# Routing attention and a bilinear feed-forward block: Strassen products for two thirds of the first batch element's up-projection, weight checks on ScalarE

## The chip, the cores and the metric

The kernel runs on one core of one Trainium2 chip. Its time is the device time in microseconds, the median of repeated runs. Before the change it is 1047.72 us (three runs, 1047.59 to 1048.28). The profile is of one execution with a span of 1045.6 us. The core has five engines with a queue each, which run side by side and wait for each other by semaphores: TensorE (PE in the profile, its weight loads PEld), VectorE (DVE), ScalarE (ACT), GpSimd (POOL) and SyncE (SP, which issues transfers here). Within a queue, instructions are worked off in order.

## What is computed

Cut to what matters, the reference is:

```python
# q, k, v: (4, 8, 768, 64), centroids: (8, 16, 64)
mask   = argmax(q_n @ c_n) [:, :, :, None] == argmax(k_n @ c_n) [:, :, None, :]
scores = where(mask, 0.125 * q @ k^T, -1e9)
attn   = softmax(scores)                      # per batch element and head
x      = (attn @ v) as (3072, 512)            # rows: batch and position
out    = ((x @ w_a) * (x @ w_b)) @ w_out      # w_a, w_b: 512 x 1536, w_out: 1536 x 512
```

The weights arrive as 64-bit floats. The kernel makes 32-bit floats of them on the chip, from the two 32-bit halves of each number.

## The kernel before

**Attention.** Four batch elements with four pairs of heads each make 16 pairs (`p`). A pair has 12 units (two halves `hf` of 384 queries, six blocks `j` of 128 keys), and two units are one group `g`, so a pair lasts 6 groups and the loop over `g` in `short_path` runs 96 of them. A group's own work is `score` (one-hot products that make the mask and q-k products into the same bank, L556), `exp` on ScalarE (L565), and, one group later, `add_up` (running sums of the exponentials, L586) and `weigh` (products with `v`, L597). Every third group `denominators` sums the exponentials over the partitions on TensorE (L620), and `normalize` inverts them (VectorE, L640 to L647) and multiplies `xT` by them (GpSimd, L652). Exponentials lie in four buffers (`pt`), scores in two.

**Clusters of the next pair.** `prep_steps` spreads them over the 6 groups of the current pair. From the fifth pair on (`by_blocks`) they are made without TensorE's transposes: VectorE transposes q and k (L477), TensorE makes the similarities in `prep_sim` (L373), VectorE transposes these (`sims_across`, L481), finds the first largest one (`assign`, L502 to L507), VectorE and GpSimd make the one-hot rows (L489, L487), VectorE transposes them (L493), and eight transfers put them into `ohT` (L497), which `score` of the pair reads.

**Feed-forward block.** For a batch element, `xT` is 512 x 768 (transposed), in four chunks of 128 and two halves of 384 columns. The up-projection makes 12 blocks `f` of 128 features. For batch elements 1 to 3, `ffn_ups` makes it by Strassen's method (Winograd's form): two blocks of features, two halves of the channels and two halves of the columns are a 2 x 2 by 2 x 2 product with seven products in place of eight. Each product is one piece of four matmuls, and each set of seven needs four combinations of weights on VectorE (S1 to S4, two chunks each, L782), four combinations of `xT` for the whole batch element (T1 to T4, L755, L767), four additions on VectorE (L815), three or four copies on ScalarE (L812) and, in every second set, three multiplications on GpSimd (L821) and one on VectorE (L864). The first batch element's up-projection is made in the plain way by `ffn_block`: a piece is eight matmuls, with one copy on ScalarE for `w_a` (L705) and one multiplication on VectorE for `w_b` (L709). `ffn_downs` (Strassen too) makes the down-projection. Matmuls of all pieces are issued at L678; the trace holds two records for each.

**Order.** The order of all queues is written out by the loop: in a group come `score`, `add_up`, the flush, `weigh`, the denominators, a step of the clusters, the rounding that is due, and then pieces of the feed-forward queue `ffn` until a credit of columns (`PER_GROUP`) is used up. After every piece one VectorE step from `todo` and one rounding that is due are put in. The first four pairs run without pieces, since no `xT` is complete yet. At the end of group 22 the first half of the first batch element is ready, and its first eight pieces are put in the queue; the others follow at the end of group 25.

**Weights.** 36 parts of 128 x 512 are loaded (two buffers `raw`). `round_w` makes a part by four VectorE instructions (L280 to L290), a size on ScalarE (L294) and an addition on GpSimd (L295). In the next group `flush_w` multiplies the part by "size at least `SMALLEST`" on VectorE (L302), which sets to zero what is too small. `due` says which part is rounded in which group: eight in the first 22 groups, the others from group 23 on, three in two groups.

**Check at the end.** `stat` holds what must stay below `LIMIT`; where it doesn't, a second program (`long_path`) computes attention again.

Of the kernel before, what the change touches and what calls it, by code (L numbers as in the profile page):

```python
# [28 lines left out]
SMALLEST = 1.125 * 2.0 ** -15  # L29

# [5 lines left out]
def kernel(  # L36
# [97 lines left out]
    with tc.If(redo > 0):  # L134
        with ExitStack() as slow:
            long_path(nc, tc, slow, c, q, k, v, out)


def short_path(nc, tc, ctx, c, cn, centroids_in, casts, n_far, q, k, v,
# [32 lines left out]
    sizep = pool("sizep", 2)  # L172
# [96 lines left out]
    flush = []  # L269

    def round_w(i):
        flush_w()
        w = w_parts[i][0]
        wi = w.bitcast(INT32)
        raw = raws.pop(i)
        halves = lambda dt: raw.bitcast(dt).rearrange("p (n two) -> p n two", two=2)
        lo, hi = halves(UINT32)[:, :, 0], halves(INT32)[:, :, 1]


        nc.vector.tensor_scalar(out=wi, in0=hi, scalar1=3, scalar2=0x3FFFFFF8,  # L280
                                op0=ALU.logical_shift_left,
                                op1=ALU.bitwise_and)
        nc.vector.scalar_tensor_tensor(out=wi, in0=hi, scalar=SIGN_TOP, in1=wi,
                                       op0=ALU.bitwise_and, op1=ALU.bitwise_or)

        rest = wtp.tile([P, WN], FP32, name="rest")
        nc.vector.tensor_scalar(out=rest.bitcast(INT32), in0=wi,
                                scalar1=SIGN_EXP, scalar2=None,
                                op0=ALU.bitwise_and)
        nc.vector.scalar_tensor_tensor(out=rest, in0=lo, scalar=2.0 ** -52,  # L290
                                       in1=rest, op0=ALU.mult, op1=ALU.mult)

        size = sizep.tile([P, WN], FP32, name="size")
        nc.scalar.activation(out=size, in_=halves(FP32)[:, :, 1], func=AF.Abs)  # L294
        nc.gpsimd.tensor_tensor(out=w, in0=w, in1=rest, op=ALU.add)  # L295
        flush.append((w, size))

    def flush_w():

        while flush:  # L300
            w, size = flush.pop(0)
            nc.vector.scalar_tensor_tensor(out=w, in0=size, scalar=SMALLEST,  # L302
                                           in1=w, op0=ALU.is_ge, op1=ALU.mult)

    stat = zero.tile([P, 4 * NPAIR], FP32, name="stat")
# [42 lines left out]
    def prep_transpose(p, i):  # L348
        if i == 0:
            qkTs[p] = qtp.tile([P, 2 * S], FP32, name="qkT")  # L350
        ps = ps_m.tile([P, 512], FP32, name="m")
        for n in range(4):
            w, j = divmod(4 * i + n, NJ)
            nc.tensor.transpose(  # L354
                out=ps[:, n * P:(n + 1) * P],
                in_=qks[p][:, w, j].rearrange("p a d -> p (a d)"),
                identity=ident)
        dst = qkTs[p][:, i * 512:(i + 1) * 512]
        if p == 0 and i == 2:
            nc.vector.tensor_copy(out=dst[:, 0:256], in_=ps[:, 0:256])  # L360
            nc.scalar.copy(out=dst[:, 256:], in_=ps[:, 256:])
        elif p == 0 and i != 1 or p == 1 and i == 2:
            nc.vector.tensor_copy(out=dst, in_=ps)
        else:
            nc.scalar.copy(out=dst, in_=ps)
# [94 lines left out]
    def prep_by_blocks(p):  # L460
# [47 lines left out]
        if p == HP:  # L508
            return [[lambda: across(0), lambda: across(1)], [sims_across],
                    assign[:2], assign[2:], [one_hot, one_hot_across], []]  # L510
# [3 lines left out]
    def prep_steps(p):  # L514
# [6 lines left out]
        if by_blocks(p):  # L521
            steps = prep_by_blocks(p)
            ready = [lambda s=s: todo.extend(s) for s in steps]
            ready[1] = both(lambda: prep_sim(p), lambda: load_v(p), ready[1])
            return ready
# [50 lines left out]
    def add_up(u):  # L576
# [6 lines left out]
        for a in range(2):  # L583
            many = p >= HP and (a == 1 or j in (2, 4))
            eng = nc.gpsimd if many else nc.vector
            eng.tensor_tensor(  # L586
                out=acc[:, a, :],
                in0=probs[u - 1][:, a, :] if j == 1 else acc[:, a, :],
                in1=probs[u][:, a, :], op=ALU.add)
# [97 lines left out]
    def ffn_block(b, blk):  # L687

        box = {}
        t0 = blk * HB  # L690

        def up(w_sb, f):
            ps = in_turn()
            for ch in range(NCH):
                in_halves(ps[:, 0:HB], w_sb[:, ch, f * P:(f + 1) * P],
                          xTs[b][:, ch, t0:t0 + HB],
# [3 lines left out]
        def piece_a(f):  # L700
            if f == 0:
                box["h"] = hp_.tile([P, NF, HB], FP32, name="h")
            ps = up(wa_sb, f)
            box["a"] = hap.tile([P, HB], FP32, name="ha")
            nc.scalar.copy(out=box["a"], in_=ps[:, 0:HB])  # L705

        def piece_b(f):
            ps = up(wb_sb, f)
            nc.vector.tensor_tensor(out=box["h"][:, f, :], in0=box["a"],  # L709
                                    in1=ps[:, 0:HB], op=ALU.mult)  # L710

        ups = [(NCH * HB, lambda f=f, piece=piece: piece(f))
               for f in range(NF) for piece in (piece_a, piece_b)]
        return ups, box
# [11 lines left out]
    def room():  # L726
        if not W:
            W["raw"] = [rawp.tile([P, 2 * WN], FP32, name="raw") for _ in range(2)]
            W["size"] = [sizep.tile([P, WN], FP32, name="size") for _ in range(2)]
            W["comb"] = combp.tile([P, 2 * P], FP32, name="comb")  # L730
        return W["raw"], W["size"], W["comb"]
# [4 lines left out]
    def up_room():  # L736
        raw, size, comb = room()
        quarter = lambda t: t[:, 0:2 * HB].rearrange("p (c t) -> p c t", c=2)
        beside = lambda t: t[:, 2 * HB:].rearrange("p (c f) -> p c f", c=2)
        chunks = lambda t: [t[:, c, :] for c in range(2)]  # L740
        W["T3"], W["T2"] = chunks(quarter(raw[0])), chunks(quarter(raw[1]))
        W["T4"] = [t[:, 0:HB] for t in size]
        W["slots"] = [chunks(beside(raw[0])), chunks(beside(raw[1])),
                      chunks(comb.rearrange("p (c f) -> p c f", c=2)),
                      [t[:, HB:] for t in size]]

    def combine_x(b):
        up_room()
        x = xTs[b]
        for c in range(2):  # L750
            x11, x12 = x[:, c, 0:HB], x[:, c, HB:S]
            x22 = x[:, c + 2, HB:S]
            t2, t3 = W["T2"][c], W["T3"][c]
            for out, l, r in ((t3, x22, x12), (x12, x12, x11), (t2, x22, x12)):
                nc.vector.tensor_tensor(out=out, in0=l, in1=r, op=ALU.subtract)  # L755

    def ffn_ups(b, h):

        x = xTs[b]
        X = {"11": [x[:, c, 0:HB] for c in (0, 1)],  # L760
             "T1": [x[:, c, HB:S] for c in (0, 1)],
             "21": [x[:, c, 0:HB] for c in (2, 3)],
             "22": [x[:, c, HB:S] for c in (2, 3)]}

        def combine_t4():
            for c in range(2):
                nc.vector.tensor_tensor(out=W["T4"][c], in0=X["21"][c],  # L767
                                        in1=W["T2"][c], op=ALU.subtract)

        def products(w_sb, i, is_a):  # L770
            N2 = NF // 2
# [13 lines left out]
            def half_1():  # L785
                combine("S1", A["21"], A["22"], ALU.add)
                combine("S2", A["S1"], A["11"], ALU.subtract)

            def half_2():
# [20 lines left out]
            def take(name, k, f):  # L810
                box[name] = place(k, f)
                nc.scalar.copy(out=box[name], in_=box["X"][:, 0:HB])  # L812

# [53 lines left out]
            return half_1, half_2, [p1, p2, p6, p5, p7, p3, p4]  # L867

        parts = [products(w_sb, i, w_sb is wa_sb) for i in range(NF // 2)
                 for w_sb in (wa_sb, wb_sb)]  # L870
        pieces = []
        for n, (half_1, half_2, ps) in enumerate(parts):
            if n == 0:
                ps[0] = both(half_1, half_2, ps[0])
                ps[2] = both(combine_t4, ps[2])
            if n + 1 < len(parts):
                ps[4] = both(ps[4], parts[n + 1][0])
                ps[6] = both(ps[6], parts[n + 1][1])
            pieces += [(2 * HB, f) for f in ps]
        return pieces  # L880
# [9 lines left out]
    def ffn_downs(b, h):  # L890
# [97 lines left out]
        def before():  # L988
            down_room()
# [19 lines left out]
    blocks = {}  # L1009

    def ffn_ready(p, hf):

        b, hp = divmod(p, HP)
        if hp < HP - 1:
            return
        if b > 0:
            if hf == 0:
                return
            h = []
            ffn.insert(len(ffn) - FREE_ROOM, (0, lambda: combine_x(b)))  # L1020
            ffn.extend(ffn_ups(b, h) + ffn_downs(b, lambda: h))
        elif hf == 0:
            blocks[0] = ffn_block(0, 0)
            ffn.extend(blocks[0][0][0:8])
        else:
            ups0, box0 = blocks[0]
            ups, box = ffn_block(0, 1)
            for n in range(3):
                ffn.extend(ups[8 * n:8 * n + 8] + ups0[8 * n + 8:8 * n + 16])
            ffn.extend(ffn_downs(0, lambda: (box0["h"], box["h"])))  # L1030
# [3 lines left out]
    GPP = UPP // 2  # L1034
# [6 lines left out]
        (UP + DOWN * 7 / 8, BG + 5.8), ((UP + DOWN) * 7 / 8, BG + 0.8),  # L1041
# [7 lines left out]
    for i in range(8, len(w_parts)):  # L1049
        due.setdefault(23 + int((i - 8) / 1.5), []).append(i)  # L1050
# [4 lines left out]
    keep_busy(12)  # L1055
    prep_transpose(0, 0)
    prep_transpose(0, 1)
# [26 lines left out]
    for g in range(NG + 3):  # L1084
# [13 lines left out]
        flush_w()  # L1098
# [7 lines left out]
        parts = due.get(g, [])  # L1106

        def round_next():
            if parts:
                i = parts.pop(0)  # L1110
                round_w(i)
                load_w(i + 2)
# [42 lines left out]
    fine = zero.tile([P, 4 * NPAIR], FP32, name="fine")  # L1155
# [15 lines left out]
def long_path(nc, tc, ctx, c, q, k, v, out):  # L1171
# [20 lines left out]
    R = 2 * NC  # L1192

# [200 lines left out]
```

## Time and profile before

| | busy us | share of the span | instructions |
|---|---|---|---|
| TensorE, matmul | 1032.8 | 99% | 7163 |
| VectorE | 657.2 | 63% | 1314 |
| GpSimd | 329.9 | 32% | 311 |
| ScalarE | 303.1 | 29% | 590 |

The first row says which engine sets the time: on the page, the chain of work that ended last is TensorE for 93% of the span and VectorE for 4%. The other rows are averages over stages that differ, so the stretch that a change touches has to be asked for by itself. The groups of instructions give a mean duration for each line: an addition of two running sums on VectorE (L586) 802 ns, a combination of weights (L782) between 285 and 644 ns, an addition to a bank's result (L815) about 550 ns, the flush (L302) 880 to 1154 ns. "Idle before" in the same rows is the time that the engine waited and for whom.

### The profile page before, as it was taken

What the parts mean: (1) busy time and instruction counts of PE and PEld (TensorE: products, weight loads), DVE (VectorE), ACT (ScalarE), POOL (GpSimd) and SP (SyncE); (2) the same over time, 40 slices, a digit from 0 to 9 for tenths busy, and PEclk for the clock granted to TensorE, in tenths of its full rate; (3) what the DMA queues carried; (4) which work ended last, traced back from release to release, by engine and by line L of the source; (5) the groups of instructions that cost most, each with busy time, mean ns of one, the idle gap of its engine ahead of it and who ended that gap; (6) DMA issues with size and microseconds to landing.
All of it is one profiled execution on the core that took longest, in us unless ns stands there. A gap on an engine that the chain in (4) does not pass through costs nothing.

```text
span 1045.6 us, 17833 instructions
## 1 busy us (share of the span) xinstructions
PE 1032.8 (99%) x7163; PEld 502.6 (48%) x7163; DVE 657.2 (63%) x1314; ACT 303.1 (29%) x590; POOL 329.9 (32%) x311
## 2 busy tenths in 40 slices
PE   9999999999999999999999999999999999999997
PEld 5444444444445554444444555444444565444564
DVE  6778877887857447555556746765454845554652
ACT  5665333233322222333323122333232201111100
POOL 1111345455543322343442422443333310211100
PEclk9999999999999999999999999999999999999999
DMA  7334343526120121203020030300000000000001
GB/s 183 87 86 86 85 106 105 125 68 144 63 49 20 40 43 23 38 5 46 4 46 3 24 66 22 49 1 20 1 4 1 11 31 21 1 1 1 2 30 34
DMA packets 120521, 46.48 MB, mean 44 GB/s; under 512 B 106608, under 2 KB 115824, under 8 KB 120432
## 3 DMA queue, kind: packets, MB, share of 16 engines
q1 hardware_dynamic: 120016, 44.85, 18.8%
q8 instruction: 58, 0.95, 0.4%
q10 hardware_dynamic: 416, 0.43, 0.1%
q14 instruction: 31, 0.25, 0.1%
HBM read 37.78 MB, written 6.29 MB: 42 GB/s over the span
## 4 chain that ended last, share of the span: by engine, by line
PE 93%; DVE 4%; issue 1%; POOL 1%; ACT 0%; DMA 0%; DVEq 0%; POOLq 0%
PE m L678 62%; PE s L556 15%; PE O L597 12%; PE s L620 1%; PE s L373 1%; PE m L620 1%; DVE raw L755 1%; PE m L373 0%; POOL xT L652 0%; DVE xT L755 0%; DMA h<-in_q_dram 0%; PE m L354 0%; DVE comb L782 0%; DVE acc L586 0%; DVE acc L647 0%
## 5 line engine op out<-in xcount | busy, mean ns | idle before, releaser
L565 ACT ACTIVATE pt<-s 128x768 f32<-128x768 f32 x192 | 145.3, 808 | 206.5 <-PE s L556 161.7
L586 POOL TENSOR_TENSOR acc<-acc,pt 128x384 f32<-128x384 f32 x144 | 152.6, 1073 | 60.2 <-ACT pt L565 43.0
L597 PE MATMUL O<-pt,v 128*64 128x384 f32 x768 | 145.0, 499 | 0.0
L556 PE MATMUL s<-qkT 64*128 64x384 f32 x768 | 139.7, 482 | 0.0
L821 POOL TENSOR_TENSOR h<-h,ha 128x384 f32<-128x384 f32 x54 | 55.5, 1030 | 258.6 <-DVE ha L815 257.7
L678 PE MATMUL m<-xT,wa_sb 128*64 128x384 f32 x672 | 117.5, 487 | 2.7 <-DVE ha L815 1.0
L678 PE MATMUL m<-xT,wb_sb 128*64 128x384 f32 x672 | 116.9, 487 | 0.0
L815 DVE TENSOR_TENSOR ha<-ha,m 128x384 f32<-128x384 f32 x72 | 39.6, 550 | 98.0 <-PE m L678 75.4
L586 DVE TENSOR_TENSOR acc<-acc,pt 128x384 f32<-128x384 f32 x96 | 74.5, 802 | 36.6 <-POOL acc L586 35.5
L815 DVE TENSOR_TENSOR h<-h,m 128x384 f32<-128x384 f32 x72 | 39.5, 548 | 80.7 <-PE m L678 53.8
L812 ACT COPY h<-m 128x384 f32<-128x384 f32 x72 | 34.5, 479 | 184.9 <-PE m L678 184.9
L597 PEld LDWEIGHTS O<-pt,v 128*64 128x64 f32 x768 | 46.6, 136 | 85.8 <-issue 80.1
L678 PE MATMUL m<-wo_sb,h 128*64 128x256 f32 x768 | 86.7, 379 | 0.0
L556 PEld LDWEIGHTS s<-qkT 64*128 64x128 f32 x768 | 70.5, 187 | 31.3 <-issue 0.2
L678 PEld LDWEIGHTS m<-xT,wa_sb 128*64 128x64 f32 x672 | 48.7, 137 | 63.4 <-issue 53.3
L678 PE MATMUL m<-raw 128*64 128x384 f32 x432 | 78.9, 486 | 0.0
L652 POOL TENSOR_TENSOR xT<-xT,acc 128x384 f32<-128x384 f32 x32 | 32.8, 1026 | 144.9 <-DVE acc L647 144.6
L678 PEld LDWEIGHTS m<-xT,wb_sb 128*64 128x64 f32 x672 | 49.0, 137 | 60.1 <-issue 56.2
L678 PEld LDWEIGHTS m<-wo_sb,h 128*64 128x64 f32 x768 | 54.9, 137 | 31.1 <-issue 5.0
L678 PE MATMUL m<-xT,h 128*64 128x256 f32 x576 | 64.5, 379 | 0.0
L678 PE MATMUL m<-xT,size 128*64 128x384 f32 x288 | 52.7, 487 | 0.0
L678 PEld LDWEIGHTS m<-xT,h 128*64 128x64 f32 x576 | 41.3, 137 | 22.3 <-issue 2.3
(169 smaller groups left out, 1302.0 us busy)
## 6 DMA issues: line engine op xcount, KB each, us to landing
raw<-in_moe_w_a_dram SPq DMA_DIRECT2D x12, 512.0 KB, 3.8
raw<-in_moe_w_b_dram SPq DMA_DIRECT2D x12, 512.0 KB, 3.6
raw<-in_moe_w_out_dram SPq DMA_DIRECT2D x12, 512.0 KB, 3.7
qk<-in_q_dram SPq DMA_DIRECT2D x48, 96.0 KB, 3.1
qk<-in_k_dram SPq DMA_DIRECT2D x48, 96.0 KB, 3.6
v<-in_v_dram SPq DMA_DIRECT2D x24, 192.0 KB, 3.8
out_dram<-rest SPq DMA_DIRECT2D x24, 128.0 KB, 1.7
v<-in_v_dram SPq DMA_DIRECT2D x4, 384.0 KB, 4.5
```

Source lines behind the costliest of these rows:

```text
L373: nc.tensor.matmul(out=ps[32 * kq:32 * kq + 32, 0:HB], lhsT=cTb[:, hp, :], rhs=qkTs[p][:, kq * HB:(kq + 1) * HB], start=True, stop=True)
L556: nc.tensor.matmul(out=s[:, a, 0:HB], lhsT=Ts[p][r, S + j * P:S + (j + 1) * P], rhs=Ts[p][r, hf * HB:(hf + 1) * HB], start=start, stop=not ...
L565: nc.scalar.activation(out=pt, in_=s[:, :, 0:HB], func=AF.Exp, scale=SCALE)
L586: eng.tensor_tensor(out=acc[:, a, :], in0=probs[u - 1][:, a, :] if j == 1 else acc[:, a, :], in1=probs[u][:, a, :], op=ALU.add)
L597: nc.tensor.matmul(out=O_of[0][a * D:(a + 1) * D, 0:HB], lhsT=vs[p][:, a, j, :], rhs=probs[u][:, a, :], start=(j == 0), stop=(j == NJ - 1))
L620: nc.tensor.matmul(out=ps[a * D:(a + 1) * D, 0:HB], lhsT=ones, rhs=t[:, a, :], start=(n == 0), stop=(n == len(terms) - 1))
L652: nc.gpsimd.tensor_tensor(out=x, in0=x, in1=den, op=ALU.mult)
L678: nc.tensor.matmul(out=ps[half], lhsT=lhsT[:, half], rhs=rhs, **kw)
L755: nc.vector.tensor_tensor(out=out, in0=l, in1=r, op=ALU.subtract)
L812: nc.scalar.copy(out=box[name], in_=box["X"][:, 0:HB])
L815: nc.vector.tensor_tensor(out=box[name], in0=box[name], in1=box[bank][:, 0:HB], op=ALU.add)
L821: nc.gpsimd.tensor_tensor(out=to, in0=to, in1=box[name], op=ALU.mult)
```

## The change

It does seven things.

- **First batch element.** Blocks 0 to 7 of its up-projection are made by `ffn_ups` (pairs 0 with 2, 1 with 3, 4 with 6, 5 with 7; 8 sets of seven products), blocks 8 to 11 in the plain way (`plain_ups`). No piece starts before both halves are ready, so all of them follow at the end of group 25. T1 to T4 lie in parts of `h` that are written later, and most of them, with S1 to S4 of the first set, are made from group 14 to group 24 (`early_steps`); T2, T3 and T4 of the second chunk are made at the end of group 25.
- **Weight check.** The flush on VectorE goes. In its place ScalarE makes the size in BF16, and a second instruction (Relu, with an accumulator) puts the amount by which sizes fall short into `stat` (`see_w`). It is put behind ScalarE's copies, and the next part's load behind it. Zeroing is done by `long_path`, if at all.
- **Rounding.** Parts from the ninth on are due from group 25, 1.45 a group.
- **Clusters.** `sims_across` of pairs from the fifth on is put in at once instead of through `todo`, which places it in front of that group's rounding; for the fifth pair the one-hot rows are made a group sooner.
- **Sums.** Of the first head's sums, VectorE makes blocks 1, 2 and 3 and GpSimd 4 and 5. Before, VectorE made 1, 3 and 5 and GpSimd 2 and 4.
- **Start.** Five matmuls fewer that only keep TensorE busy, and the first copies of the transposes go to ScalarE, the last to VectorE.
- **Later batch elements.** The combinations of `xT` come in two steps instead of one, those of the weights in three instead of two.

```diff
+        unseen.append((i, halves(FP32)[:, :, 1]))
-    def flush_w():
-        while flush:
-            w, size = flush.pop(0)
-            nc.vector.scalar_tensor_tensor(out=w, in0=size, scalar=SMALLEST,
-                                           in1=w, op0=ALU.is_ge, op1=ALU.mult)
+    def see_w():
+        while unseen:
+            i, upper = unseen.pop()
+            size = spare()[1].bitcast(BF16)[:, WN:2 * WN]
+            nc.scalar.activation(out=size, in_=upper, func=AF.Abs)
+            n = 4 * NPAIR + i
+            nc.scalar.activation(out=size, in_=size, func=AF.Relu, scale=-STEEP,
+                                 bias=edge[:, 0:1], accum_out=stat[:, n:n + 1])
+            load_w(i + 2)
...
-        if p == 0 and i == 2:
-            nc.vector.tensor_copy(out=dst[:, 0:256], in_=ps[:, 0:256])
-            nc.scalar.copy(out=dst[:, 256:], in_=ps[:, 256:])
-        elif p == 0 and i != 1 or p == 1 and i == 2:
+        if p < 2 and i == 2:
             nc.vector.tensor_copy(out=dst, in_=ps)
...
         if p == HP:
-            return [[lambda: across(0), lambda: across(1)], [sims_across],
-                    assign[:2], assign[2:], [one_hot, one_hot_across], []]
+            return [[lambda: across(0), lambda: across(1)],
+                    [sims_across] + assign[:2], assign[2:] + [one_hot],
+                    [one_hot_across], [], []]
...
-            ready[1] = both(lambda: prep_sim(p), lambda: load_v(p), ready[1])
+            ready[1] = both(lambda: prep_sim(p), lambda: load_v(p), steps[1][0],
+                            lambda: todo.extend(steps[1][1:]))
...
-            many = p >= HP and (a == 1 or j in (2, 4))
+            many = p >= HP and (a == 1 or j > 3)
...
+        return {HP * GPP - 10: both(begin, T("T1", 0)), HP * GPP - 8: T("T1", 1),
+                HP * GPP - 4: T("T3", 0), HP * GPP - 3: T("T2", 0),
+                HP * GPP - 2: T("T4", 0),
+                HP * GPP - 1: lambda: [f() for f in combinations[0:2]],
+                HP * GPP: lambda: combinations[2]()}
...
-        elif hf == 0:
-            blocks[0] = ffn_block(0, 0)
-            ffn.extend(blocks[0][0][0:8])
         else:
-            ups0, box0 = blocks[0]
-            ups, box = ffn_block(0, 1)
-            for n in range(3):
-                ffn.extend(ups[8 * n:8 * n + 8] + ups0[8 * n + 8:8 * n + 16])
-            ffn.extend(ffn_downs(0, lambda: (box0["h"], box["h"])))
+            h = h_first
+            for name in ("T3", "T2", "T4"):
+                combination_x(0, name, 1)
+            ffn.extend(ups_first + plain_ups(0, h, range(NF - 4, NF)))
+        ffn.extend(ffn_downs(b, lambda: h))
...
-        (UP + DOWN * 7 / 8, BG + 5.8), ((UP + DOWN) * 7 / 8, BG + 0.8),
+        (UP * 11 / 12 + DOWN * 7 / 8, BG + 2.8), ((UP + DOWN) * 7 / 8, BG + 0.8),
...
-        due.setdefault(23 + int((i - 8) / 1.5), []).append(i)
+        due.setdefault(25 + int((i - 8) / 1.45), []).append(i)
...
-    keep_busy(12)
+    keep_busy(5)
     prep_transpose(0, 0)
+    keep_busy(2)
...
-        flush_w()
```

## The prediction

> **What bounds the kernel now.** I read the page's busy times and chain first, then the table of stages, then who waited in the stage that the change rebuilds. The page:
>
> ```profile
> PE 1032.8 (99%) x7163; PEld 502.6 (48%) x7163; DVE 657.2 (63%) x1314; ACT 303.1 (29%) x590; POOL 329.9 (32%) x311
> PE 93%; DVE 4%; issue 1%; POOL 1%; ACT 0%; DMA 0%; DVEq 0%; POOLq 0%
> ```
>
> TensorE is busy for all but 13 us and is 93% of the chain, so time comes from fewer matmuls or fewer waits of TensorE, and VectorE work counts only where TensorE waits for it. Three stages (us from the start: groups 21 to 25; the first batch element's feed-forward beside attention; the second's, by Strassen, beside attention):
>
> ```profile
> 97.30:139.30 42.00, 39.70 (x244) 18.27 (x244) 33.42 (x60) 16.79 (x32) 10.68 (x9) 1.00 0.42 101
> 139.30:302.50 163.20, 163.20 (x1022) 70.53 (x1023) 131.23 (x200) 55.71 (x105) 87.47 (x75) 1.00 0.34 90
> 398.80:560.70 161.90, 161.40 (x1016) 69.45 (x1016) 92.31 (x200) 50.10 (x98) 60.18 (x59) 1.00 0.16 26
> ```
>
> Columns: length, then busy PE, PEld, DVE, ACT, POOL. Only in the first does TensorE lose time; in the second VectorE is busy for 80%, with rounding and plain pieces; in the third 57%, with Strassen pieces and no rounding. The change puts Strassen pieces and rounding together. TensorE's waits in the first:
>
> ```profile
> PE s L556 <- DVE sim L481: 1.0, 1, 1.0
> PE m L678 <- POOL xT L652: 0.9, 1, 0.9
> ...
> PE s L620 <- DVE acc L586: 0.5, 1, 0.5
> ```
>
> With a 0.5 us wait that shows only on the weight load (below), and some 0.6 us of spacing around these, about 3.5 us. The timeline of group 19 (from 91.7) to 21 shows what VectorE has in front of the sums that the denominators need:
>
> ```profile
> 90.96 0.42 DVE L280 TENSOR_SCALAR wa_sb<-raw 128x512 int32<-128x512 int32 x1
> ...
> 94.78 0.85 PE L373 MATMUL m<-qkT,cTb 128*32 128x384 f32 x8
> ...
> 95.70 0.58 DVE L481 STREAM_TRANSPOSE sim<-m 128x384 f32<-128x384 f32 x1 [2.41 <-PE m L373]
> ...
> 101.85 1.02 DVE L586 TENSOR_TENSOR acc<-acc,pt 128x384 f32<-128x384 f32 x2
> ...
> 102.46 0.19 PEld L620 LDWEIGHTS m<-acc,ones 128*64 128x64 f32 x2 [0.52 <-DVE acc L586]
> ```
>
> VectorE rounds a part (90.96 to 93.29) while TensorE is still before the similarities, then waits 2.41 us for them, and comes to the sums of group 20 at 101.85, when TensorE stands ready for them at 102.4.
>
> **What the Trainium skill says.** *SBUF — State Buffer*, "Who interferes with whom": VectorE's second port pair is GpSimd's, under an exclusive lock. The trace agrees: of 288 weight combinations (L782) the 205 that lie beside no GpSimd instruction have a median of 284 ns, the other 83 a mean of 745; additions from a bank (L815) stay at 544 to 554 ns. *ScalarE: Activation LUTs*, "Table sets: the hidden batching unit": relu and abs are in every set, so the new Relu needs no table load; the trace has two loads (1283 ns each), both at the start, with Abs among the exponentials ever after. *TensorE: Matmul & The Clock Gate*, "What's actually happening": the clock is granted by activity in windows of about 3.4 us; five idle matmuls fewer at the start (at 175 ns) leave a hole under 0.4 us, so I expect the page's PEclk row to stay at 9s; no run here shows it yet.
>
> **The change part by part.**
>
> *Strassen products.* Before: 48 pieces of 8 matmuls, 384. After: 8 sets x 7 products x 4 = 224, and 16 plain pieces x 8 = 128; 352. The 32 that go are 64 records; the chain has 32 records of L678 in 5.16 us, 161 ns each. **-10.3 us**, on the bounding engine.
>
> *Old waits.* The first pieces no longer wait for GpSimd's L652 at 112.9, and `sims_across` is in time for its bank: **-3.5 us**, with new waits counted below.
>
> *Flush gone.* 36 x 0.88 to 1.15 us of VectorE. In the first 90 us the flush delays sums by 0.68 us, and denominators at 27.9, 53.4 and 78.8 start about 0.36 us late; at the third an early T takes its place. **-0.7 us.** In its place ScalarE gets a Relu (0.68 us, as Abs, by the trace) and an accumulator read (0.2) per part: 32 us on an engine at 29%. Behind it stand exponentials and copies; the scores' two buffers cover one such delay. 0.
>
> *Start.* VectorE, the chain there, loses a copy (L363, 0.69 us) between L117 and the centroids; similarities end about **0.4 us** sooner.
>
> *Later batch elements.* TensorE waits 0.5 us at 397 and 646 because additions of the down-projection (L939) stand behind six `xT` combinations at once. In two steps: **-0.8 us.** The new split of sums takes away 35.5 us of VectorE's waits for GpSimd over the whole run; beyond the first batch element TensorE waits for VectorE at four places of 0.5 us only, so 0. GpSimd has seven sums per half pair as before.
>
> *Group 19, sims_across at once.* It now stands in front of the rounding, so VectorE, done with its sums at 91.04, idles until 95.70, and the rounding comes after. From there in its new order: similarities 0.58, rounding 2.33, maximum and comparison 1.14, normalize 1.42, four sums 2.73, rank and first 1.15, one-hot 0.57, T3 0.56 (L755 undisturbed), first sum of group 20 0.51: 106.7. TensorE needs that sum at 102.4: **+4.3 us.**
>
> *ohT.* L493 then ends at 107.8; eight issues (110.26 to 115.29 before, 5.03 us) and 1.8 us to landing give 114.7. TensorE, from 107.4 after the denominators through two groups without pieces (3.16 us each), is at group 24's scores at 113.7: **+1.0 us** (0 to 3). Before, six pieces filled that time.
>
> *Group 25 and the first set.* After the similarities' product VectorE has 0.58, two roundings 4.66, normalize 1.42, GpSimd's L652 with hand-over 1.2, T3 and T2 0.56 each: 9.0 us to T2. TensorE has 3.16 us of attention and two products (2.58): 5.7. The third product (S2 by T2) waits **+3.3 us**. VectorE enters the next group late, and with a rounding between additions the second set's bank Y comes about **1.1 us** late.
>
> *Groups 29 to 37, Strassen beside rounding.* Six groups of VectorE: 9 roundings 21.0, 32 weight combinations at 0.36 = 11.5, 17 additions 9.1, six sums 4.2, clusters 8.1 with L477, normalize 2.8, others 1.1: 57.8 us. TensorE: 6 x 3.16, 29 pieces at 1.29, denominators and similarities 2.1: 58.5, and 59.5 as the third stage above spaces them. VectorE is at 97%, and banks come free in its order. Lower end 0, upper end (combinations at the mean of 745 ns, 12 us more in six groups, for nine groups) 16. I take **+2 us**, near the lower end, since the split of sums frees waits there (17 us in the second stage).
>
> Sum: -10.3 -3.5 -0.7 -0.4 -0.8 +4.3 +1.0 +3.3 +1.1 +2.0 = **-4.0 us: 1043.7.**
>
> **Rivals.** (A) *VectorE keeps up.* The waits in groups 19 to 27 shrink to some 2 us, since VectorE gains the flush and the sums' waits, and the products' gain stays: -15.7 + 2 gives 1034. For it: VectorE's 80% in the second stage holds 26.8 us of flush. Against: the waits of groups 19 and 25 follow from queue order, not from load. (B) *VectorE becomes the bound.* The lock doubles combinations while GpSimd has sums, roundings and the sets' multiplications: the upper end of 16 us in place of 2, less the overlap of the two late starts with it (about 5), gives -4 + 14 - 5 = +5, 1052, slower. (C) *Half of that*: the stretch costs 5 us, 1046.7, within 0.2%.
>
> **How the numbers follow.** Forecast 0.50 (1041 to 1045.6), A 0.20, C 0.17, B 0.13. Faster by over 0.2% (below 1045.6): 0.70; same (to 1049.8): 0.17; slower: 0.13. The range 1036 to 1050 leaves out the lower half of A and B's upper part.
>
> **What would show it.** 64 records of L678 fewer. A wait of TensorE's denominators for VectorE's sums of about 4 us near 102; one for T2 (an `h` tile) of about 3 us near 130; idle time of VectorE for L373's product in group 19 near 4.6 us. Two table loads still. In the stage of groups 29 to 37, VectorE near 95% busy and TensorE's waits for it 1 to 5 us. If TensorE has no waits of over 1 us before 140, the two queue-order steps are wrong and A holds; if the waits in 150 to 250 exceed 8 us, B. If instead ScalarE's copies stand behind `see_w` and hold TensorE, a step I put at 0 is wrong.

## The result and the profile after

The changed kernel takes 1061.24 us (median of four runs, 1060.81 to 1063.36), 1.0132 times the kernel before, 95% interval 1.0115 to 1.015. It is slower by 13.5 us; 1043.7 was forecast. The profile is of the longest of the four executions (1063.36 us at a mean granted clock of 0.988; the other three had 0.991), so it shows some 2 us more than the median. The page after, answering to the two lines shown of before, with the clock's row, where each digit is a fortieth of the span:

```profile
PE 1032.2 (97%) x7094; PEld 498.3 (47%) x7094; DVE 682.4 (64%) x1370; ACT 336.4 (32%) x674; POOL 344.1 (32%) x323
PEclk9999889989999999999999999999999999999999
PE 89%; DVE 8%; ACT 1%; issue 1%; POOL 0%; DMA 0%; DVEq 0%; POOLq 0%; ACTq 0%
```

TensorE's records went from 7163 to 7094, yet its busy time stayed (1032.8, now 1032.2). Fewer matmuls took as long, so some ran slower: the clock's row has four 8s, from four stretches in which the granted clock was 0.5 (from 109.9, 137.2 and 232.8 us for 6.8 us each, and from 202.1 us for 3.4 us; 23.9 us in all). The last 2 to 3 us of the span are at 0.5 too, in the kernel before as well. And VectorE's share of the chain rose from 4% to 8%.

The table of stages after, columns as before. The first line is groups 21 to 25, the second the feed-forward block from group 26 to the end of group 35, the third from there into group 42, the fourth the second batch element's stage:

```profile
101.70:129.30 27.60, 22.64 (x128) 9.12 (x128) 23.08 (x44) 12.59 (x25) 7.02 (x6) 0.88 0.32 70
129.30:248.20 118.90, 106.31 (x616) 43.70 (x612) 109.62 (x188) 51.51 (x106) 60.24 (x54) 0.93 0.33 87
248.20:308.00 59.80, 59.80 (x380) 26.15 (x380) 49.86 (x75) 28.03 (x57) 34.83 (x31) 1.00 0.36 92
413.60:575.50 161.90, 161.90 (x1020) 70.04 (x1018) 91.75 (x208) 50.04 (x98) 59.72 (x58) 1.00 0.15 26
```

The second line is the loss. VectorE, 80% busy in the stage that this replaces, is at 92% (109.62 of 118.90), and TensorE is idle for 12.6 us and at a clock of 0.93. In the third and fourth TensorE is busy throughout. TensorE's largest waits over the whole run:

```profile
PE m L686 <- DVE ha L841: 7.9, 5, 3.3
PE m L628 <- DVE acc L594: 5.2, 2, 5.0
PE m L686 <- ACT h L837: 3.9, 1, 3.9
PE s L563 <- ACT pt L572: 2.0, 6, 0.4
```

The columns after the colon are us in total, times, longest. Line 628 of the changed kernel is the denominators, 594 the sums, 841 VectorE's addition to a Strassen tile, 837 ScalarE's copy `take`, 686 the pieces' matmuls. The timeline from group 19 on answers to the one of before:

```profile
94.94 1.45 PE L563 MATMUL s<-qkT 64*128 64x384 f32 x8
...
98.69 0.58 DVE L486 STREAM_TRANSPOSE sim<-m 128x384 f32<-128x384 f32 x1 [4.71 <-PE m L378]
99.19 0.38 DVE L280 TENSOR_SCALAR wa_sb<-raw 128x512 int32<-128x512 int32 x1
...
104.77 0.82 PE L628 MATMUL m<-pt,ones 128*64 128x384 f32 x4
...
109.96 1.01 DVE L594 TENSOR_TENSOR acc<-acc,pt 128x384 f32<-128x384 f32 x2
110.55 2.01 PE L628 MATMUL m<-acc,ones 128*64 128x384 f32 x4 [4.96 <-DVE acc L594]
...
113.10 2.77 PE L563 MATMUL s<-qkT 64*128 64x384 f32 x8
```

VectorE idles 4.71 us for the similarities and only then rounds, and the sums come at 109.96. TensorE waits 4.96 us, and then its four matmuls take 2.01 us in place of the 0.82 us of the same form at 104.77; the eight score products behind them take 2.77 us, in group 19 1.45. The granted clock is 0.5 there.

### The profile page after: what moved, and what is told of

Read it like the earlier page. It is cut to its first block, busy times and chain, and to the rows that moved or that the text cites. A ratio compares the mean times of both kernels' runs of the same rounds, so it can differ in the third digit from the quotient of the medians.

```text
span 1061.4 us, 17953 instructions
## 1 busy us (share of the span) xinstructions
PE 1032.2 (97%) x7094; PEld 498.3 (47%) x7094; DVE 682.4 (64%) x1370; ACT 336.4 (32%) x674; POOL 344.1 (32%) x323
## 3 DMA queue, kind: packets, MB, share of 16 engines
q1 hardware_dynamic: 120016, 44.85, 18.3%
## 4 chain that ended last, share of the span: by engine, by line
PE 89%; DVE 8%; ACT 1%; issue 1%; POOL 0%; DMA 0%; DVEq 0%; POOLq 0%; ACTq 0%
PE m L686 59%; PE s L563 14%; PE O L605 11%; PE s L628 1%; PE m L628 1%; PE s L378 1%; DVE pair L805 1%; ACT pt L572 1%; DVE rest L290 1%; PE m L378 1%; DVE comb L805 0%; DVE acc L594 0%; DVE rest L287 0%; PE m L362 0%; DVE ha L841 0%
## 5 line engine op out<-in xcount | busy, mean ns | idle before, releaser
L847 POOL TENSOR_TENSOR h<-h,ha 128x384 f32<-128x384 f32 x66 | 68.4, 1039 | 262.3 <-DVE ha L841 261.8
L841 DVE TENSOR_TENSOR ha<-ha,m 128x384 f32<-128x384 f32 x88 | 48.0, 547 | 104.7 <-PE m L686 77.6
L837 ACT COPY h<-m 128x384 f32<-128x384 f32 x88 | 42.1, 478 | 211.6 <-PE m L686 211.6
L841 DVE TENSOR_TENSOR h<-h,m 128x384 f32<-128x384 f32 x88 | 48.1, 546 | 78.1 <-PE m L686 50.9
L686 PE MATMUL m<-xT,wa_sb 128*64 128x384 f32 x480 | 85.8, 498 | 7.9 <-DVE ha L841 7.9
L686 PE MATMUL m<-xT,wb_sb 128*64 128x384 f32 x480 | 83.3, 487 | 0.7 <-DVE h L841 0.7
L837 ACT COPY ha<-m 128x384 f32<-128x384 f32 x66 | 31.5, 477 | 100.0 <-PE m L686 100.0
L594 DVE TENSOR_TENSOR acc<-acc,pt 128x384 f32<-128x384 f32 x96 | 58.7, 638 | 5.1 <-ACT pt L572 3.8
L686 PEld LDWEIGHTS m<-xT,wa_sb 128*64 128x64 f32 x480 | 34.1, 138 | 53.4 <-issue 37.5
L686 PEld LDWEIGHTS m<-xT,wb_sb 128*64 128x64 f32 x480 | 34.4, 137 | 43.9 <-issue 37.0
```

The source lines that it names most:

```text
L594: eng.tensor_tensor(out=acc[:, a, :], in0=probs[u - 1][:, a, :] if j == 1 else acc[:, a, :], in1=probs[u][:, a, :], op=ALU.add)
L686: nc.tensor.matmul(out=ps[half], lhsT=lhsT[:, half], rhs=rhs, **kw)
L841: nc.vector.tensor_tensor(out=box[name], in0=box[name], in1=box[bank][:, 0:HB], op=ALU.add)
L847: nc.gpsimd.tensor_tensor(out=to, in0=to, in1=box[name], op=ALU.mult)
```

## The experiments

All are made from the changed kernel. Times before ran beside them at 1047.8 to 1048.2 us.

**e1, `sims_across` back behind the rounding.**

```diff
-            ready[1] = both(lambda: prep_sim(p), lambda: load_v(p), steps[1][0],
-                            lambda: todo.extend(steps[1][1:]))
+            ready[1] = both(lambda: prep_sim(p), lambda: load_v(p), ready[1])
```

> The changed kernel with one thing undone: sims_across of the pairs from the fifth on goes through todo again, behind that group's rounding. Theory 1 (queue order in front of group 20's sums): the 5.0 us wait of the denominators (L628) for VectorE's sums at 110.5 shrinks to under 1 us, the stretch of half clock behind it (6.8 us, 3.4 us of work) goes, and 1 to 3 us of waits for the similarities' bank come back: 1053 to 1057. Rival (VectorE's load, not its order, is the loss): the wait only moves to another place, 1060 to 1062.

1054.15 us, 7.1 less than with the change, as the first theory had it in size. The wait of the denominators is 2.2 us in place of 5.0, not under 1, and 3.4 us at half clock stay behind it. The 3.9 us wait for ScalarE's copy at 139 went too, down to 0.4, which was not expected. With the change, VectorE idles 4.27 us in group 25 for the similarities and has two roundings and the normalize after them; ScalarE's `check_inverses` waits 4.86 us for that normalize, and `see_w` and the copy stand behind it. So that wait, too, came in good part from VectorE's queue. The lines of the changed kernel:

```profile
129.40 0.58 DVE L486 STREAM_TRANSPOSE sim<-m 128x384 f32<-128x384 f32 x1 [4.27 <-PE m L378]
...
136.88 0.21 ACT L668 ACTIVATE inv<-inv 128x12 f32<-128x12 f32 x1 [4.86 <-DVE acc L655]
...
138.49 0.46 ACT L837 COPY h<-m 128x384 f32<-128x384 f32 x1
...
139.00 3.23 PE L686 MATMUL m<-h,pair 128*64 128x384 f32 x8 [3.92 <-ACT h L837]
```

What did not go are the waits in the Strassen stretch. This is the list of TensorE's waits of e1 from 120 to 250 us:

```profile
PE m L685 <- DVE ha L840: 7.8, 5, 3.8
PE m L685 <- DVE h L840: 2.3, 1, 2.3
PE m L685 <- DVE h L772: 0.8, 1, 0.8
PE m L685 <- ACT h L836: 0.4, 1, 0.4
```

**e9, the same for the fifth pair only.**

```diff
+            if p == HP:
+                ready[1] = both(lambda: prep_sim(p), lambda: load_v(p), ready[1])
```

> The changed kernel with sims_across through todo for the fifth pair only (group 19); for later pairs it stays in front of the rounding. If the loss by its place is the one wait of group 21 with its half clock, this is worth as much as e1: 1053 to 1056. Rival (later pairs, where VectorE has no time left, pay for it too): half of e1's gain, 1057 to 1059.

1057.54 us: 3.7 of e1's 7.1. The rival holds: the place of this one transpose costs about as much at the later pairs as at group 19. ScalarE's copy is again late by 3.9 us.

**e2, no weight check on ScalarE.**

```diff
-            nc.scalar.activation(out=size, in_=upper, func=AF.Abs)
-            nc.scalar.activation(out=size, in_=size, func=AF.Relu, scale=-STEEP,
-                                 bias=edge[:, 0:1], accum_out=stat[:, n:n + 1])
```

> The changed kernel without ScalarE's weight check: Abs, Relu and accumulator of see_w are left out (the weights are not checked), only the next part's load stays there. Theory 2 (ScalarE's queue is the loss): the 3 us lost before group 19 come back, the 3.9 us wait for take at 139 shrinks to under 2 us and the half clock behind it (3.4 us of work) goes: 1051 to 1055. Rival (all of the loss is VectorE's): under 2 us, 1059 to 1061.

1058.09 us, 3.2 less: between the two theories. Group 19 starts 0.4 us after before's in place of 3.0, so the check costs 2.6 us by delays of exponentials and copies in the first four pairs; TensorE's six waits for exponentials there (2.0 us in all, the last line of the waits above) are gone. After that it gains little: the wait for the copy falls from 3.9 to 2.5, and one of 2.2 for T2 (`h`) comes in its place.

**e3, plain pieces for the whole first batch element**, with before's due groups of rounding; the other edits stay.

```diff
-            ffn.extend(ups_first + plain_ups(0, h, range(NF - 4, NF)))
+            blocks[0] = ffn_block(0, 0)
+            ffn.extend(blocks[0][0][0:8])
...
+                ffn.extend(ups[8 * n:8 * n + 8] + ups0[8 * n + 8:8 * n + 16])
```

> The changed kernel with the first batch element's up-projection and the due groups of rounding as before the change (plain pieces, first ones from group 22 on), all else kept, the weight check behind ScalarE's copies. Strassen beside rounding is the loss: the waits for VectorE's additions in 150 to 245 (8.6 us), two half clock stretches there (5.1 us of work), the wait at 139 and the half clock behind it (7.3 us) go, 10.3 us of matmuls come back: about 1050. Rival (order and ScalarE's check are the loss, Strassen gains): 1065 to 1071.

1051.32 us. The waits of 150 to 245 are gone, every one; what is left is a wait of 4.5 us at group 21 with its half clock. So Strassen for these eight blocks with its start at group 26, though it saves 10.3 us of matmuls, makes the kernel 9.9 us longer.

**e4, TensorE kept busy in its two long waits.**

```diff
         ps = apart()
+        if (p, hf) == (3, 0):
+            for _ in range(28):
+                nc.tensor.transpose(out=ps[:, HB:HB + P], in_=ident, identity=ident)
...
             def p6():
+                if not b and i == 0 and is_a:
+                    for _ in range(22):
+                        nc.tensor.transpose(out=box["Z"][:, HB:HB + P],
+                                            in_=ident, identity=ident)
```

> The changed kernel with TensorE kept busy in its two long waits: 28 transposes that nothing reads (4.9 us at 175 ns) in front of the denominators of group 21, and 22 (3.9 us) in front of the third product of the first set. The waits for VectorE and ScalarE stay. Theory 3 (a wait of 4 to 5 us also halves the clock for 6.8 us): both stretches of half clock go, 3.4 us each, 1053 to 1056. Rival (the clock falls for another reason, or the stretches cost nothing since other engines bound there): 1060 to 1063.

1058.36 us, 2.9 less; 5 to 8 us were expected. In the profiled execution, 1057.67 us, all four stretches of half clock are gone, also the two that had no filler near them. (The 28 transposes took 3.3 us, not 4.9, so a part of the first wait was left.) Against the profiled execution of the changed kernel it is 5.7 us shorter, of the 12 us of work that 23.9 us at half clock hold back. The other three executions of e4 had mean granted clocks of 0.992, 0.996 and 0.996, so in them part of the half clock was still there, and the medians compare 0.991 with 0.996. The largest waits of e4 from 97 to 255 us, with the clock's row of its page:

```profile
PEclk9999999999999999999999999999999999999999
```

```profile
PE m L689 <- DVE ha L844: 9.4, 5, 3.3
PE m L689 <- DVE h L844: 2.3, 1, 2.3
PE m L631 <- DVE acc L594: 1.6, 1, 1.6
```

In the Strassen stretch TensorE at full clock just comes sooner to the same late VectorE: its waits for additions grew from 8.6 to 11.7 us. So the half clock follows from the waits, and only part of the work that it holds back shows in the time: about half, as an estimate, from 5.7 us of 12 between the profiled executions, and from 2.9 us of some 5 (0.005 of the span) between the medians.

**e6, rounding cut to its first instruction from the ninth part on** (made from e1).

```diff
+        if i >= 8:
+            unseen.append((i, halves(FP32)[:, :, 1]))
+            return
         nc.vector.scalar_tensor_tensor(out=wi, in0=hi, scalar=SIGN_TOP, in1=wi,
```

> e1 (the changed kernel, sims_across through todo) with rounding cut from the ninth part on: only its first VectorE instruction (L280) is left, so those weights are wrong; three VectorE instructions of 1.8 us in all and GpSimd's addition per part are left out. If VectorE's load in groups 26 to 37 is the loss, the waits for its additions (10 us) and the half clock at 190 (3.4 us) go: 1040 to 1044. Rival (waits from the order in the queues or from ScalarE): 1050 to 1054.

1038.34 us, 15.8 less than e1: no wait over 0.5 us is left after group 21. Strassen gains when VectorE has no rounding beside it. This alone does not say whether it was the rounding's own time or the lock on the port that VectorE shares with GpSimd.

**e7, VectorE's work kept, GpSimd's nearly emptied** (made from e1): 16 columns in its addition of the low bits, in its sums and in its multiplications of the sets.

```diff
+        few = slice(0, WN if i < 8 else 16)
...
+            few = slice(0, 16 if many and p < HP + 4 and j > 1 else HB)
...
+                    few = slice(0, HB if b else 16)
```

> e1 with GpSimd's instructions kept but nearly emptied (16 columns in place of 384 or 512) for the first batch element: its sums of pairs 4 to 7, its addition of the low bits from the ninth part on, its multiplications in the sets, so sums, weights and products are wrong. VectorE has as many instructions as in e1. If the shared port makes VectorE's weight combinations long (714 ns mean in place of 280), they fall to under 350 ns, some 17 us of VectorE come free and the waits of 150 to 245 go: 1040 to 1044. Rival (VectorE's own instructions fill it): combinations stay over 550 ns, 1050 to 1054.

1039.41 us, 14.7 less than e1, with as many VectorE instructions (1370). VectorE does not gain by waiting less for GpSimd's results: from group 29 to 37 of e1 it waits 1.3 us for them. Its instructions became shorter: its busy time in these groups falls from 92.1 to 68.7 us, most of it in the weight combinations (31.0 us for 46 of them, then 11.5 for 41). By form, these are, in the changed kernel from 139 to 248 us and then in e7 from 130 to 235 us:

```profile
L805 DVE TENSOR_TENSOR pair<-wb_sb 128x128 f32<-128x128 f32 x14 | 9.7, 731 | 0.0
L805 DVE TENSOR_TENSOR comb<-wa_sb 128x128 f32<-128x128 f32 x6 | 5.5, 961 | 0.0
L805 DVE TENSOR_TENSOR pair<-comb,wa_sb 128x128 f32<-128x128 f32 x6 | 4.7, 822 | 0.0
```

```profile
L807 DVE TENSOR_TENSOR pair<-wb_sb 128x128 f32<-128x128 f32 x16 | 4.6, 326 | 0.0
L807 DVE TENSOR_TENSOR comb<-wa_sb 128x128 f32<-128x128 f32 x6 | 1.6, 305 | 0.0
L807 DVE TENSOR_TENSOR pair<-comb,wa_sb 128x128 f32<-128x128 f32 x6 | 1.6, 299 | 0.0
```

The number before the last bar is the mean in ns. The same instructions take two to three times as long beside GpSimd's work. Counted from the starts and ends in the changed kernel's trace, 10 of 50 combinations overlap no GpSimd instruction and take 280 ns; the other 40 have a mean of 800. All 56 of e7 have a mean of 332. The additions from a bank (L841) have a mean of 537 ns alone and of 535 beside GpSimd. The Trainium skill says the same in *SBUF — State Buffer*, "Who interferes with whom": a VectorE instruction with two inputs from SBUF contends with a GpSimd instruction that reads SBUF, and the shared ports are an exclusive lock.

**e5, e3 with `sims_across` and the fifth pair's clusters as before the change; e10, e3 with only the first of the two.**

```diff
-            return [[lambda: across(0), lambda: across(1)],
-                    [sims_across] + assign[:2], assign[2:] + [one_hot],
-                    [one_hot_across], [], []]
+            return [[lambda: across(0), lambda: across(1)], [sims_across],
+                    assign[:2], assign[2:], [one_hot, one_hot_across], []]
```

> The run with plain pieces (e3), and in addition sims_across through todo and the fifth pair's clusters a group later, as before the change. What remains of the change: weight check on ScalarE, split of sums, start, later batch elements. If queue order explains e3's one long wait (4.5 us at the denominators of group 21) and the half clock behind it (3.4 us of work): 1051.3 - 4.5 - 3.4 = 1043 to 1046, under before. Rival (those sums are late for VectorE's load): 1049 to 1052.

> e3 (plain pieces) with only sims_across through todo; the fifth pair's one-hot rows stay a group sooner. Between e3 (1051.3) and e5 (1045.75) it divides their 5.6 us: if the place of sims_across is all of it, 1045 to 1046.5; if the sooner one-hot row (0.55 us of VectorE in front of group 20's sums) has a part, 1047 to 1049.

e5 takes 1045.75 us, 0.9979 times before (0.997 to 0.9988), and e10 1047.1. So of e3's 5.6 us the place of `sims_across` makes 4.2, and the sooner one-hot row 1.4: TensorE waits 1.7 us in e10 for the sums of group 20, which have one more VectorE instruction in front of them.

**e8, twelve parts rounded early, the rest at 1.2 a group** (made from e1, with the clusters of e5).

```diff
-    due = {3 * i + 1: [i] for i in range(8)}
-        due.setdefault(25 + int((i - 8) / 1.45), []).append(i)
+    due = {2 * i + 1: [i] for i in range(12)}
+        due.setdefault(25 + int((i - 12) / 1.2), []).append(i)
```

> e1, with the fifth pair's clusters a group later as before the change, and twelve instead of eight parts rounded in the first 24 groups and the others at 1.2 instead of 1.45 a group from group 25. In groups 26 to 37 VectorE has a fifth less rounding: 2.7 parts of 2.3 us, 6 us. If its load is the loss: 1054 - 2 (wait at group 21) - 6 + 1.5 (four more checks on ScalarE early) = 1046 to 1049. Rival: 1053 to 1056.

1053.78 us, no gain. TensorE's waits for additions fell from 10.1 to 4.7 us, as the load theory has it, but 5.3 us of waits for the `ohT` transfers (L561) took their place: with the clusters a group later and no pieces before group 26, nothing hides them. From the start of group 28 to that of group 38 it loses 7.6 us against before, where e1 loses 16.7, but from group 21 to 28 it falls 5.8 us behind e1, and loses 2.5 us more than e1 after group 38. Two edits at once made this run say less than it could.

**e12, four sets in place of eight, with plain pieces between them** (made from e1).

```diff
-        N2, firsts = (NF // 2, range(NF // 2)) if b else (2, (0, 1, 4, 5))
+        N2, firsts = (NF // 2, range(NF // 2)) if b else (2, (0, 1))
...
+            ffn.extend(ups_first[:14] + f4 + one + f5 + two_ + f67)
```

> e1 with Strassen for blocks 0 to 3 only (4 sets in place of 8), plain pieces for 4 to 11, four of them between sets with the next set's weight combinations beside them; rounding due from group 24. 5.2 us of matmuls come back. If VectorE's load per piece is the loss: waits of 150 to 245 fall from 10 us to under 3 and their half clock goes: 1054.2 + 5.2 - 7 - 3.4 = 1047 to 1050. Rival (any set beside rounding makes TensorE wait): 1052 to 1056.

1053.64 us, a miss. After 150 us TensorE has no wait over 1 us, so the sets with plain pieces between them are carried. But rounding a group sooner met the first sets: waits of 2.2 us at the denominators of group 21, 2.0 at group 25's similarities, 2.2 for T2 and 3.9 for an addition that stands behind two roundings.

**e11, e5 with the check of the first eight parts on VectorE**, which multiplies each by it in the next group.

```diff
+        if i >= 8:
             unseen.append((i, halves(FP32)[:, :, 1]))
+            return
+        size = spare()[0]
+        nc.scalar.activation(out=size, in_=halves(FP32)[:, :, 1], func=AF.Abs)
+        flush.append((w, size))
```

> e5 with the weight check of the first eight parts on VectorE (size on ScalarE, flush, as before the change), of the others on ScalarE. If ScalarE's second instruction is what costs 2.65 us before group 19, of which 0.9 us is left from group 25 on: 1044 to 1045.2. Rival (nothing is left of it, or the flush costs as much): 1045.4 to 1046.5.

1043.65 us, 0.9959 times before (0.9945 to 0.9973): the fastest of the versions that leave nothing out. All groups from the first to the 24th start 0.4 us before those of the kernel before, as group 0 already does, so ScalarE no longer delays the first pairs. Its waits from 97 to 255 us are these two:

```profile
PE s L574 <- DVE sim L499: 1.0, 1, 1.0
PE m L697 <- POOL xT L671: 0.9, 1, 0.9
```

**e13, e11 with four sets behind plain pieces and rounding slower beside them.**

```diff
-        due.setdefault(25 + int((i - 8) / 1.45), []).append(i)
+        n = 23 + int((i - 8) / 1.9) if i < 16 else 27 + int((i - 15) / 1.25)
+        due.setdefault(n, []).append(i)
...
+            ffn.extend(ups + ups_first + plain_ups(0, h, range(NF - 4, NF)))
```

> e11 with Strassen for blocks 4 to 7 of the first batch element (4 sets): the plain pieces of blocks 0 to 3 come first (half of them from group 22 on), then the sets, then the plain pieces of blocks 8 to 11; parts 9 to 16 are rounded at 1.9 a group beside plain pieces, the rest at 1.25 a group beside the sets. 5.2 us of matmuls fewer than e11. If e12's 10 us of waits came from its first set standing beside two roundings in a row, and sets beside slower rounding fit on VectorE: waits under 3 us, 1043.65 - 5.2 + 2.5 = 1039 to 1042. Rival (a set beside any rounding makes TensorE wait some 1.5 us): 1043 to 1047.

1044.04 us, the same as e11 within what can be told, in the rival's range. VectorE is busy for 19.62 of the 20 us from 200 to 220. Of the 5.2 us of matmuls saved, 3.8 go to waits (5.7 from 97 to 255 us, 1.9 in e11), and 0.5 us is lost to e11 at group 16, where an early T combination lies (another 0.5 us is there at group 0 already). So the fault is not only in the start: even four sets at a slower rate only pay for themselves.

## Why the prediction was wrong

The forecast was -4.0 us and the result +13.5. By its own steps:

- *Strassen products, -10.3*: right. The records of the pieces fell by 64, from 4800 to 4736, and e6, which has the sets without the load beside them, is 7.4 us faster than e5 although it keeps a wait of 2.2 us and 3.4 us at half clock (1.7 us of work) at group 21. That makes 11.3 if these are taken off, and 9.5 if two old waits (1.0 and 0.8 us) that e5 alone has are too.
- *Groups 29 to 37, Strassen beside rounding, +2.0*: **this is the step that failed.** It put VectorE's work at less than TensorE's. From the start of group 28 to that of group 38 the changed kernel loses 18.3 us against before, and e1 16.7; the two versions made from e1, e7 and e6, lose 6.0 and 4.8 in the same groups, as before had its first eight pieces done in groups 23 to 25. So VectorE's load, under the lock, costs e1 10.7 to 11.9 us there. The sign that was named for rival B, waits of over 8 us from 150 to 250, came too. The term that was mis-sized is "32 weight combinations at 0.36". 0.36 is the average over the whole run before (102.2 us of busy time for 288), in which 205 of 288 ran beside no GpSimd instruction. In the third stage of before it is 0.40 (35.7 us for 90), with VectorE at 57% and GpSimd at 37%. In the changed kernel from 139 to 248 us it is 0.65 (32.4 us for 50; their records overlap a little, so that their mean length is 0.70), with VectorE at 93% and GpSimd at 51%: GpSimd's additions come right behind every rounding, and 40 of 50 combinations met GpSimd. With 0.65 the sum for six groups is 57.8 + 32 x 0.29 = 67.1 us, against TensorE's 59.5: 7.6 us over in six groups, 11.4 in nine, within what the runs showed. The upper end of the step, 16 us, and rival B named this; the choice of a place near the lower end was wrong, and the 17 us of VectorE's waits for GpSimd that the new split of sums frees did not make up for it.
- *Group 19, +4.3*: right in place and size, 4.96 us. e10 adds that the sooner one-hot row has 1.4 us of such a wait. *Group 25, +3.3*: 3.9 us, the size right, the path only in part, so there is luck in it. The profile names ScalarE's copy, behind the weight check, where T2 was forecast; e1 shows that the same late VectorE is behind it, and without the check (e2) the copy is waited for 2.5 us and T2 2.2.
- *Waits counted one to one, the clock staying at 9s*: wrong. Waits of 5.0, 3.9 and 3.3 us, and two of 2.0 and 1.0 close together, came with 23.9 us at half clock. By e4 its price is 2.9 us between the medians and 5.7 between the profiled executions. The Trainium skill's *TensorE: Matmul & The Clock Gate*, "What's actually happening", gives windows of about 3.4 us; the stretches here are 3.4 or 6.8 us long, and which waits start one differs: 3.3 us did in the changed kernel and did not in e4, and 2.2 us at the denominators of group 21 did in e1, e6, e7 and e9 and did not in e12.
- *ScalarE's check at 0, the flush gone at -0.7*: wrong sign. It costs 2.6 us before group 19, 3.2 in all (e2), and moving the first eight checks back to VectorE gives 2.1 (e5 to e11). "The scores' two buffers cover one such delay" was the failing sentence: ScalarE was 59% busy in the first 100 us, not 29%, and copies for the one-hot rows stand in its queue too. That the Relu needs no table load was right: the trace after has the same two loads at the start.
- *ohT, +1.0*: no such wait came; TensorE was late itself. *Bank Y, +1.1*: one wait of 0.7. *Start -0.4, later batch elements -0.8*: group 0 starts 0.2 us sooner in this trace, but 0.5 sooner to 0.2 later in the other versions, which start in the same way, so this is not shown; from group 53 to the end 1.4 us are gained. *Old waits, -3.5*: gone as forecast, replaced by those above; but the prediction's own first row has TensorE idle for only 2.3 us there (42.00 less 39.70), so the step was some 1.2 us too high.

The stretch at 10.7 to 11.9 in place of 2, ScalarE at 3.2 in place of -0.7, and the half clock at 2.9 in place of 0 give 15.5 to 16.7 of the 17.5 us by which the forecast was off. These sums overlap: e1 has 6.8 us at half clock within the stretch, and a delay taken away in one place comes back in the next. How the last few us divide among them stays open.

## What to carry to other kernels

A duration averaged over stages in which VectorE and GpSimd leave each other room does not hold in a stage where both are busy. Before summing up VectorE's work for a stage, ask of each instruction that the trace shows longer beside GpSimd how much GpSimd work will run beside it, and if the sum comes near the bound (here 57.8 of 59.5 us), take the price under overlap. How much of the rise is due to VectorE's own load and how much to GpSimd's was not separated here. Work moved away from TensorE pays only while the engine that takes the extra work has room; here eight sets lost 9.9 us, four only paid for themselves, and none, with those small edits kept that pay (e11), gained some 4 us. And a share of the whole span (ScalarE at 29%) says nothing of the stage in which the new work lands.

## What the runs showed of the hardware

An addition of 128 x 128 with both inputs from SBUF took 280 ns alone, and 800 on average beside a GpSimd instruction, which is the price of the lock. The average hides two cases: 12 of the 40 took 267 to 286 ns, as if alone, and 28 took 616 to 1385. An addition with a bank as one input showed no such price (537 and 535 ns). But it is not a matter of two SBUF inputs alone: the first instruction of the rounding (L280, 128 x 512, int32) has one, and in the changed kernel took 412 ns on average alone (22 of 36) and 949 beside GpSimd (14).

Half clock comes in stretches of 3.4 or 6.8 us after waits of some 2 to 5 us, not after each of them, and makes eight score products 2.77 us long in place of 1.45. With TensorE kept busy in two of the waits (e4), one execution had no such stretch before its last 2 to 3 us, not even behind the two waits that were left without a filler; the other three had mean clocks of 0.992 to 0.996. What decides it is explained by no run here.
